# A fused linear-attention and SwiGLU kernel: the opening batch taken whole, and the hand-overs between batches rearranged

## The chip, the cores and the metric

The kernel runs on one core of a Trainium2 chip. A core has a matrix engine (PE, with its weight loads, PEld), a vector engine (DVE), an activation engine (ACT), a general engine (POOL) and a queue engine (SP); transfers between memory and the on-chip memory (SBUF) are issued from the queues of SP, ACT and POOL and moved by 16 DMA engines. Products land in PSUM, of which this program uses eight banks of 2 KB per partition. The metric is device microseconds of one execution; lower is better. Each engine works through its own instructions in the order in which the program gives them and waits on semaphores for the others.

## What is computed

Eight batches of 576 rows, eight heads of 64. For each batch and head the 64 x 64 matrix of k and v is summed over the rows, each row of q is multiplied by it, and the result is scaled to unit mean square and by g_norm. The heads side by side make 512 columns per row (4608 rows in all), and a gated feed-forward layer with its own norm follows.

```python
kv = np.einsum('bhsd,bhse->bhde', k, v)
out = np.einsum('bhsd,bhde->bhse', q, kv)
rms = np.sqrt(np.mean(out * out, axis=-1, keepdims=True) + 1e-06)
attn = out / rms * g_norm
x = attn.transpose(0, 2, 1, 3).reshape(B * S, H * D)
xn = x / np.sqrt(np.mean(x * x, axis=-1, keepdims=True) + 1e-06) * rms_g
g = xn @ w_gate
result = (g * sigmoid(g) * (xn @ w_val)) @ w_out
```

## The kernel before

Rows go through the layer in nine blocks of 512: block n below 8 is the first 512 rows of batch n ("batch n" from here on), block 8 is the eight tails of 64 rows. All products are in bf16. For a batch, `kv_products` makes the four 128 x 128 head-pair products on PE (20 matmuls, five row chunks each), `kv_copy` keeps their diagonal blocks in `kv_all`, `o` gives 128 rows of attention output (four matmuls), and from their squares `sums` forms the sum and the weighted sum for each row and head. `chain` turns both norms into one factor per row and head: twelve small DVE operations, with two steps of a root iteration. `scale` multiplies the rows by it (tile `xna`), and they are transposed into `xnt`, by four DMA transposes on SP (`x_rows`) or on PE (`x_turn`, with a copy out of PSUM).

The layer itself (`Ffn`) is 12 up units and 4 down products. `up(j)` is four matmuls into `g_ps` and four into `v_ps` (two banks each), a silu on ACT and a product on DVE into `h_sb`; `down(c)` is 12 matmuls into `o_ps`, a copy on ACT into `o_sb`, and every second time an output transfer on SP. The weights come as fp32 into staging slots (`st`, seven of 8 KB per partition, used in turn) and are rounded to bf16 by `round_w`, with the norm gain in it, and `round_wo`. q, k and v come the same way and are rounded by `cast_piece` and `cast_tail`.

The order is written out by hand: the program text is the order on every engine. Three stretches differ.

- **Opening.** Batch 0 is done in two halves of 256 rows (`Open`, q loaded in two halves). For each head pair come a cast of k on DVE, one of v on ACT, the products, two copies into `kv_all`, a product that gives the output with heads on the partitions (`outT`), and its square on ACT; sums are then tiny matmuls with the matrix `sel`. The rows are copied to SBUF (`outa`) and scaled from there. The first four up units run on the first half, then on the second, and weights are rounded between units.
- **Batch 0's down, batch 1's attention.** `wo` rounding, casts of q, the turning of q on PE, `o` and `sums` of batch 1 (squares on ACT, a product and two reductions on DVE for each tile) lie between parts of the down products. SP's queue then holds the output transfer of batch 0's first half, the loads of batch 2 (k, v, q), the second output transfer and the loads of batch 3.
- **Batches 1 to 7.** `steps` hangs work for the next batch behind each of the 16 units (0 to 11 up, 12 to 15 down): in batch 1 the chain behind unit 12, with two tiles of `x_rows` there and two behind unit 13; from batch 2 on the chain behind unit 10, and the tiles behind units 11 and 12.

On DVE the chain stands in the same queue as each unit's product into `h_sb`, which the down products read.

Of the kernel before, what the change touches and what calls it, by code (L numbers as in the profile page):

```python
# [17 lines left out]
def kernel(  # L18
# [19 lines left out]
    T = 4  # L38
# [38 lines left out]
    gnorm_bc = consts.tile([128, D], FP32, name="gnorm_bc")  # L77
# [63 lines left out]
    def load_w(blk):  # L141
        j0, j1 = W_BLOCKS[blk]
        for name, view in (("g", wg_view), ("v", wv_view)):
            st = stage()
            ap = st[:, 0 : NS * (j1 - j0) * 128].rearrange("p (s f) -> p s f", s=NS)
            nc.sync.dma_start(out=ap, in_=view[:, :, j0 * 128 : j1 * 128])
            w_st[name, blk] = ap
# [160 lines left out]
    class Ffn:  # L308
# [29 lines left out]
        def down_out(self, c):  # L338
# [10 lines left out]
            elif c % 2 == 1:  # L349
                if n == 0:  # L350
                    r0 = 256 * (c // 2)
                    rows = out[r0 : r0 + 256, :].rearrange("(p t) d -> p t d", t=2)
                else:
                    rows = out[n * S : n * S + MAIN, :].rearrange("(p t) d -> p t d", t=T)[:, c - 1 : c + 1, :]
                nc.sync.dma_start(out=rows, in_=self.o_sb)
# [6 lines left out]
    q0 = stage().rearrange("p (f h x) -> p f h x", f=2, h=H)  # L362
    k0, v0 = stage(), stage()
    raws[0, "k"], raws[0, "v"] = k0, v0

    def q0_view(f, hs):
        return q[0, hs, 256 * f : 256 * f + 256, :].rearrange("h (p t) d -> p h (t d)", t=2)

    nc.sync.dma_start(out=q0[:, 0, 0:4, :], in_=q0_view(0, slice(0, 4)))
    nc.scalar.dma_start(out=q0[:, 0, 4:8, :], in_=q0_view(0, slice(4, 8)))  # L370
    load_tail("k", k, 0, nc.sync)
    load_tail("v", v, 0, nc.scalar)
    for j in range(NS):
        hs = slice(2 * j, 2 * j + 2)
        for queue, st, src in ((nc.sync, k0, k), (nc.scalar, v0, v)):
            queue.dma_start(
                out=st.rearrange("p (h x) -> p h x", h=H)[:, hs, :], in_=main_view(src, 0)[:, hs, :]
            )
    nc.scalar.preload_act_table(ACT.Silu)
    nc.sync.dma_start(out=q0[:, 1], in_=q0_view(1, slice(0, 8)))  # L380
# [5 lines left out]
    nc.gpsimd.dma_start(out=gnorm_bc, in_=g_norm.partition_broadcast(128))  # L386
# [4 lines left out]
    nc.vector.memset(sel, 0.0)  # L391
    nc.vector.memset(kv_all, 0.0)
    for i in range(2):
        nc.vector.memset(sel[i * D : (i + 1) * D, 0, i : i + 1], 1.0 / D)
    warm_sb = consts.tile([128, 256], BF16, name="warm_sb")
    nc.vector.memset(warm_sb, 0.0)

# [4 lines left out]
    for blk in range(len(W_BLOCKS)):  # L402
        load_w(blk)

    gam_ps = att_pool.tile([128, 8], FP32, name="att_ps")
    nc.tensor.matmul(gam_ps[:, 0:5], lhsT=gam[0:5, :], rhs=ident32[0:5, 0:5], is_transpose=True, start=True, stop=True)
    nc.vector.tensor_copy(out=gcol, in_=gam_ps[:, NS : NS + 1])
    nc.vector.tensor_scalar(
        out=rowscale, in0=gam_ps[:, 0:NS], scalar1=gcol[:, 0:1], scalar2=None, op0=OP.mult
    )  # L410
    for i in range(2):
        ps_ = slice(i * D, (i + 1) * D)
        nc.vector.scalar_tensor_tensor(
            out=sel[ps_, 1, i : i + 1], in0=gcol[ps_, :], scalar=1.0 / d_model, in1=gcol[ps_, :],
            op0=OP.mult, op1=OP.mult,
        )

    alloc_q(0)
    qb0 = bufs[0]["q"]
    qt0 = qt_pool.tile([128, NS, MAIN], BF16, name="qt")  # L420

    def q0_cast(f, half, engine):
        hs = slice(4 * half, 4 * half + 4)
        cast(engine, qb0[:, 2 * f : 2 * f + 2, hs, :], q0[:, f, hs, :].rearrange("p h (t d) -> p t h d", t=2))

    def q0_turn(f, engines):
        ps = ops_pool.tile([128, NS, 2, 128], BF16, name="o_ps")
        for j in range(NS):
            for i in range(2):
                nc.tensor.matmul(  # L430
                    ps[:, j, i, :], lhsT=qb0[:, 2 * f + i, 2 * j : 2 * j + 2, :], rhs=identity,
                    is_transpose=True, start=(i == 0 and j == 0), stop=(i == 1 and j == NS - 1),
                )
        for half, engine in enumerate(engines):
            js = slice(2 * half, 2 * half + 2)
            cast(engine, qt0[:, js, 256 * f : 256 * f + 256], ps[:, js].rearrange("p j i t -> p j (i t)"))

    q0_cast(0, 0, nc.vector)
    q0_cast(0, 1, nc.vector)
    q0_turn(0, (nc.vector, nc.scalar))  # L440
    cast_tail(0, "k", nc.vector)
    cast_tail(0, "v", nc.scalar)

    class Open:
        def __init__(self, f):
            self.f = f
            self.sq = consts.tile([128, NS, 256], BF16, name=f"sqT{f}")
            self.banks = {}

        def outT(self, j):  # L450
            pool_, nm = ((gps_pool, "g_ps"), (vps_pool, "v_ps"))[j // 2]
            self.banks[j] = pool_.tile([128, MAIN], FP32, name=nm)
            nc.tensor.matmul(
                self.banks[j][:, 0:256], lhsT=kv_all[:, 0, j, :], rhs=qt0[:, j, 256 * self.f : 256 * self.f + 256],
                start=True, stop=True,
            )

        def square(self, j):
            nc.scalar.activation(out=self.sq[:, j, :], in_=self.banks[j][:, 0:256], func=ACT.Square)
# [286 lines left out]
```

## Time and profile before

| | us |
|---|---|
| three runs: median (lowest to highest) | 369.72 (366.54 to 371.88) |
| the profiled execution | 372.12 |
| its span, first to last instruction | 370.3 |
| PE busy in the span | 325.9 (88%) |
| DVE, ACT busy | 192.3, 189.3 |
| POOL busy | 8.7 |
| mean granted clock of PE | 0.97 |

The page's forty slices show where PE is not busy and where the clock falls; each digit is a tenth, a slice is 9.3 us.

```profile
PE   0567997586989799999999999999999999999995
PEld 0345643342444344445445444544454444444442
DVE  3367565256439426825781684278157716752320
ACT  1354665450656935395648556653955444513321
POOL 5000000000000000000000003000000000000000
PEclk9999998887899989999999999999999999999999
DMA  7999680029960469057715922790570153022013
```

The gaps of PE and the eights and sevens of the clock all lie in the first 14 slices, that is in the first 130 us; DMA is nearly full in the first five and again in slices 10 and 11. Rows of other views stand where the prediction uses them. In them a line gives start, duration, engine, line of the program, operation, output and inputs with their shapes, a count, and in brackets the idle time ahead and what ended it.

### The profile page before, as it was taken

The numbers are of one execution on the slowest core, as the hardware profiler recorded it, in microseconds if no ns is written. First come the engines' busy times: TensorE is split into PE (matmuls) and PEld (weight loads), VectorE is DVE, ScalarE is ACT, GpSimd is POOL, SyncE is SP. The second block draws the span as 40 slices with busy tenths as digits, with TensorE's granted clock in tenths as the row PEclk, the third lists the DMA queues.
The fourth block names the chain that finished last, engine by engine and source line by source line (L and its number), as shares of the span: only waits on it lengthen the run. The fifth ranks groups of instructions, "written<-read, shape, count | busy, mean of one in ns | idle before, by whom it ended". The sixth has DMA issues, their size and how long they took to land.

```text
span 370.3 us, 4813 instructions
## 1 busy us (share of the span) xinstructions
PE 325.9 (88%) x1717; PEld 161.6 (44%) x1749; DVE 192.3 (52%) x439; ACT 189.3 (51%) x349; POOL 8.7 (2%) x18
## 2 busy tenths in 40 slices
PE   0567997586989799999999999999999999999995
PEld 0345643342444344445445444544454444444442
DVE  3367565256439426825781684278157716752320
ACT  1354665450656935395648556653955444513321
POOL 5000000000000000000000003000000000000000
PEclk9999998887899989999999999999999999999999
DMA  7999680029960469057715922790570153022013
GB/s 180 366 339 343 207 313 17 0 73 370 379 86 3 113 170 311 4 135 210 251 25 148 337 89 58 176 354 10 139 186 19 28 153 104 1 57 115 0 25 89
DMA packets 80327, 55.39 MB, mean 150 GB/s; under 512 B 46492, under 2 KB 74144, under 8 KB 80304
## 3 DMA queue, kind: packets, MB, share of 16 engines
q1 hardware_dynamic: 78032, 53.62, 48.4%
q10 hardware_dynamic: 2144, 1.44, 1.3%
q0 software_dynamic: 128, 0.04, 0.4%
q8 instruction: 13, 0.21, 0.2%
q14 instruction: 10, 0.08, 0.1%
HBM read 37.78 MB, written 9.44 MB: 128 GB/s over the span
## 4 chain that ended last, share of the span: by engine, by line
PE 58%; DVE 11%; ACT 3%; issue 2%; SPq 2%; DMA 1%; DVEq 0%
PE v_ps L321 19%; PE g_ps L321 19%; PE o_ps L333 16%; DVE h_sb L327 3%; PE att_ps L258 2%; PE att_ps L219 2%; SPq L651 1%; DVE ssq L273 1%; ACT o_sb L341 1%; DVE sa L190 1%; DVE sc L192 1%; ACT vb L95 1%; DVE wsq L272 1%; ACT kb L95 1%; DVE sr L174 1%
## 5 line engine op out<-in xcount | busy, mean ns | idle before, releaser
L327 DVE TENSOR_TENSOR h_sb<-silu,v_ps 128x512 bf16<-128x512 bf16 (+1 forms) x112 | 74.6, 666 | 129.7 <-PE v_ps L321 79.2
L321 PE MATMUL g_ps<-xnt,wg_sb 128*128 128x512 bf16 (+1 forms) x428 | 113.7, 385 | 4.3 <-DMA xnt<-xna 2.9
L321 PE MATMUL v_ps<-xnt,wv_sb 128*128 128x512 bf16 (+1 forms) x446 | 114.9, 381 | 0.5
L333 PE MATMUL o_ps<-wo_sb,h_sb 128*128 128x512 bf16 x422 | 99.8, 390 | 10.3 <-ACT wo_sb L95 5.5
L326 ACT ACTIVATE silu<-g_ps 128x512 bf16<-128x512 f32 (+1 forms) x112 | 65.6, 586 | 76.9 <-PE g_ps L321 71.6
L333 PEld LDWEIGHTS <-h_sb 128*128 128x128 bf16 x432 | 42.5, 100 | 63.9 <-issue 11.6
L321 PEld LDWEIGHTS <-wv_sb 128*128 128x128 bf16 x448 | 45.3, 101 | 51.9 <-issue 2.8
L321 PEld LDWEIGHTS <-wg_sb 128*128 128x128 bf16 x448 | 43.5, 101 | 46.1 <-DMA xnt<-xna 3.4
L341 ACT COPY o_sb<-o_ps 128x512 f32<-128x512 f32 x36 | 21.0, 587 | 43.0 <-PE o_ps L333 42.8
L263 ACT ACTIVATE sq<-att_ps 128x512 bf16<-128x512 f32 x32 | 19.1, 598 | 23.9 <-PE att_ps L258 23.1
L273 DVE TENSOR_REDUCE ssq<-sq 128x8 f32<-128x512 bf16 x32 | 21.7, 679 | 0.0
L274 DVE TENSOR_REDUCE wssq<-wsq 128x8 f32<-128x512 bf16 x32 | 21.6, 676 | 0.0
L283 DVE TENSOR_TENSOR xna<-outa,sy 128x512 bf16<-128x512 bf16 x32 | 19.9, 685 | 0.1
L265 ACT CAST outa<-att_ps 128x512 bf16<-128x512 f32 x32 | 18.6, 582 | 0.0
L95 ACT CAST vb<-st 128x512 bf16<-128x512 f32 x32 | 18.5, 615 | 0.0
L272 DVE TENSOR_TENSOR wsq<-sq,gsq 128x512 bf16<-128x512 bf16 x32 | 13.4, 419 | 4.3 <-ACT sq L263 4.3
L95 ACT CAST qb<-st 128x512 bf16<-128x512 f32 x26 | 14.3, 618 | 1.7 <-DMA st<-in_q_dram 1.7
L219 PE MATMUL att_ps<-vb,kb 128*128 128x128 bf16 x140 | 10.3, 219 | 2.2 <-DVE kb L97 1.3
L258 PEld LDWEIGHTS <-qt 128*128 128x128 bf16 x112 | 9.0, 102 | 6.5 <-issue 0.6
L219 PEld LDWEIGHTS <-kb 128*128 128x128 bf16 x140 | 9.0, 98 | 5.7 <-DVE kb L97 1.5
L258 PE MATMUL att_ps<-kv_all,qt 128*128 128x128 bf16 x112 | 11.2, 226 | 0.0
L95 ACT CAST kb<-st 128x512 bf16<-128x512 f32 x20 | 10.9, 619 | 0.0
(94 smaller groups left out, 137.2 us busy)
## 6 DMA issues: line engine op xcount, KB each, us to landing
out_dram<-o_sb SPq DMA_DIRECT2D x16, 512.0 KB, 3.1
st<-in_k_dram SPq DMA_DIRECT2D x7, 1024.0 KB, 8.5
st<-in_v_dram SPq DMA_DIRECT2D x7, 1024.0 KB, 8.8
st<-in_q_dram SPq DMA_DIRECT2D x7, 1024.0 KB, 6.6
st<-in_moe_w_out_dram SPq DMA_DIRECT2D x3, 1024.0 KB, 6.1
st<-in_moe_w_gate_dram SPq DMA_DIRECT2D x2, 1024.0 KB, 6.4
st<-in_moe_w_val_dram SPq DMA_DIRECT2D x2, 1024.0 KB, 6.2
rawt<-in_k_dram SPq DMA_DIRECT2D x8, 128.0 KB, 8.2
```

Of the source, the lines that this page charges most:

```text
L95: engine.copy(out=dst, in_=src)
L219: nc.tensor.matmul(self.kv_ps[:, j, :], lhsT=bufs[n]["k"][:, c, hs, :], rhs=bufs[n]["v"][:, c, hs, :], start=(j == 0 and c == 0), stop=(j ...
L258: nc.tensor.matmul(ps[:, 2 * j : 2 * j + 2, :], lhsT=a, rhs=b, start=(j == 0 and i == 0), stop=(j == NS - 1 and i == len(terms) - 1),)
L263: nc.scalar.activation(out=self.sq, in_=ps, func=ACT.Square)
L273: nc.vector.reduce_sum(out=self.ssq[:, c, :], in_=self.sq, axis=AX.X)
L274: nc.vector.reduce_sum(out=self.wssq[:, c, :], in_=wsq, axis=AX.X)
L283: nc.vector.tensor_tensor(out=self.xna[c], in0=self.outa[c], in1=self.alpha[:, c, :].to_broadcast([128, H, D]), op=OP.mult)
L321: nc.tensor.matmul(ps[:, 0:w], lhsT=wt[:, s, j * 128 : (j + 1) * 128], rhs=x[:, s, lo:hi], start=(s == 0), stop=(s == NS - 1),)
L326: nc.scalar.activation(out=silu[:, 0:w], in_=g_ps[:, 0:w], func=ACT.Silu)
L327: nc.vector.tensor_tensor(out=self.h[:, j, lo:hi], in0=silu[:, 0:w], in1=v_ps[:, 0:w], op=OP.mult)
L333: nc.tensor.matmul(self.o_ps[c], lhsT=self.h[:, j, c * 128 : (c + 1) * 128], rhs=wo_sb[:, j, :], start=(j == 0), stop=(j == NF - 1),)
L341: nc.scalar.copy(out=self.o_sb[:, c % 2, :], in_=self.o_ps[c])
```

## The change

It touches seven places.

1. **Loads.** q, k and v of batch 0 come in the layout of all other batches, by pieces of four and two heads instead of two (q's pieces were 512 bytes wide, now 1024); the two smallest weight blocks share one staging slot each for gate and value, so that two slots are freed; batch 1's q is asked for before `wo`.
2. **Opening whole.** `Early` replaces `Open`: all 512 rows of q are turned at once, products over 512 columns for squares, one set of sums, one chain of 32 columns. A mask and one multiplication replace two copies into `kv_all`. `scale` reads the rows from PSUM; `outa` is gone here.
3. **Casts issued ahead.** ACT casts the next v ahead of a square. Sixteen idle matmuls (`warm`) follow the last `o`. Up units 0 and 1 run on 128, 128 and 256 rows; the rest on 512.
4. **Roundings.** Value block 0 and block 1 go to POOL; block 2 is rounded in one run ahead of unit 2, block 3 in units 4 to 6; k and v of batch 1 are cast in units 7 to 10, q on POOL.
5. **Second batch by products.** Batch 1 takes its sums as batch 0 does (`out_turned`, `square`, `sums`) and scales from PSUM, its `o` in the `g_ps` and `v_ps` banks; `wo` is rounded by ACT and DVE (block 0), POOL and DVE (1), POOL and ACT (2).
6. **Batch 1's steps.** Casts for batch 2 by a table (q and k in the first two units, v after), `o` and `sums` one unit earlier.
7. **The chain.** In every batch from 1 on, chain, the four scales and the four DMA transposes stand behind up unit 11.

```diff
     def load_w(blk):
         j0, j1 = W_BLOCKS[blk]
+        size = NS * (j1 - j0) * 128
+        shared = stage() if size <= 1024 else None
...
+        def out_turned(self, j, pool_, name):
+            ps = pool_.tile([128, MAIN], FP32, name=name)
+            nc.tensor.matmul(ps, lhsT=kv_all[:, self.n, j, :], rhs=self.qt[:, j, :], start=True, stop=True)
+            return ps
...
+        def scale(self, c):
+            self.xs[c] = xna_pool.tile([128, H, D], BF16, name="xna")
+            nc.vector.tensor_tensor(
+                out=self.xs[c], in0=self.o_ps[c], in1=self.alpha[:, c, :].to_broadcast([128, H, D]), op=OP.mult
+            )
...
+    for s in range(NS):
+        round_w(0, "v", s, nc.gpsimd)
+    for name in "gv":
+        for s in range(NS):
+            round_w(1, name, s, nc.gpsimd)
+    warm(vps_pool.tile([128, MAIN], FP32, name="v_ps"), 16)
...
+    ffn = Ffn(0)
+    load_batch(1, "kvq")
+    for c in range(3):
+        first.scale(c)
+        if c < 2:
+            first.turn((c,), ops_pool, "o_ps", nc.scalar)
+        if c == 0:
+            p = Up(ffn, 0, 0, 128)
+            p.products()
+            p.silu()
...
+    att.kv_products((0, 1))
+    att.kv_products((2, 3))
+    att.kv_copy()
+    round_wo(0, 0, nc.scalar)
+    round_wo(0, 1, nc.vector)
+    att.q_turn(0, nc.scalar)
+    att.q_turn(1, nc.vector)
+    second.qt = att.qt
+    for c in range(2):
+        ffn.down_products(c, 0, 4)
+    round_wo(1, 0, nc.gpsimd)
+    round_wo(1, 1, nc.vector)
+    for j in range(NS):
+        second.square(j, second.out_turned(j, att_pool, "att_ps"))
+    for c in range(2):
+        ffn.down_products(c, 4, 8)
+    round_wo(2, 0, nc.gpsimd)
+    round_wo(2, 1, nc.scalar)
+    for j in range(NS):
+        second.sums(j, att_pool, "att_ps")
+    second.chain()
+    for c in range(T):
+        second.o(c, *(((gps_pool, "g_ps"), (vps_pool, "v_ps"))[c // 2]))
+    for c in range(2):
+        ffn.down_products(c, 8, NF)
+    for c in range(2):
+        ffn.down_out(c)
+    ffn.down_products(2, 0, NF)
...
+            plan = {
+                0: ("q0", "q1", "k0", "k1"),
+                1: ("q2", "q3", "k2", "k3"),
+                2: ("v0", "v1", "k4"),
...
-            steps[10] += [nxt.chain]
-            for c in range(2):
+            steps[11].append(nxt.chain)
+            for c in range(T):
                 steps[11] += [lambda c=c: nxt.scale(c), lambda c=c: nxt.x_rows(c)]
-                steps[12] += [lambda c=c: nxt.scale(2 + c), lambda c=c: nxt.x_rows(2 + c)]
```

What this does to the order is shown at three places; a row is line, operation, output and inputs with the tile names used above. First ACT in the opening, from its first cast on. Before:

```order
L95 COPY qt<-o_ps 128x2x256
L95 CAST vb_119<-rawt 64x512
L95 CAST vb_119<-st 128x4x128
L459 ACTIVATE sqT_205<-g_ps 128x256
L95 CAST vb_119<-st 128x4x128
L459 ACTIVATE sqT_205<-g_ps 128x256
L95 CAST vb_119<-st 128x4x128
L459 ACTIVATE sqT_205<-v_ps 128x256
L95 CAST vb_119<-st 128x4x128
L459 ACTIVATE sqT_205<-v_ps 128x256
L481 CAST outa<-o_ps 128x512 x2
```

And now:

```order
L99 CAST qb<-st 128x4x256
L99 CAST vb_123<-rawt 64x512
L99 CAST vb_123<-st 128x4x128
L99 COPY qt<-o_ps 128x1024
L99 CAST vb_123<-st 128x4x128
L425 ACTIVATE sqT<-g_ps 128x512
L99 CAST vb_123<-st 128x4x128
L425 ACTIVATE sqT<-g_ps 128x512
L99 CAST vb_123<-st 128x4x128
L425 ACTIVATE sqT<-v_ps 128x512 x2
L160 ACTIVATE wg_sb<-st,rowscale 128x256 x4
```

The cast of the second piece of v has moved ahead of the first square, and each later cast likewise; half of q's cast and of its copy has come to ACT, and the copies of the rows are gone.

Second, POOL from its last fill of the opening (`vb`) to the fill of the staging slots for the tails of q. Before:

```order
L390 MEMSET kb_117 64x512
L390 MEMSET kb_118 64x512
L390 MEMSET vb_119 64x512
L390 MEMSET vb_120 64x512
L644 MEMSET st 64x2048 x2
```

And now:

```order
L392 MEMSET vb_124 64x512
L162 TENSOR_SCALAR wv_sb<-st,rowscale 128x256 x4
L162 TENSOR_SCALAR wg_sb<-st,rowscale 128x256 x4
L162 TENSOR_SCALAR wv_sb<-st,rowscale 128x256 x4
L101 CAST qb<-st 128x4x128 x4
L101 CAST wo_sb<-st 128x1024 x2
L715 MEMSET st 64x2048 x2
```

POOL, which had no arithmetic, has twelve roundings, four casts of q and two of `wo`.

Third, DVE at the end of a batch's up units, batch 2 as an example: the end of the chain and what follows it, before,

```order
L190 TENSOR_TENSOR sa_1555<-sy_1553 128x32
L192 SCALAR_TENSOR_TENSOR sc_1557<-sa_1555,sz 128x32
L194 SCALAR_TENSOR_TENSOR sy_1559<-sc_1557,sy_1553 128x32
L327 TENSOR_TENSOR h_sb<-silu,v_ps 128x512
L283 TENSOR_TENSOR xna<-outa,sy_1559 128x512 x4
```

and now the last two products into `h_sb` and the start of the chain:

```order
L333 TENSOR_TENSOR h_sb<-silu,v_ps 128x512 x2
L284 TENSOR_SCALAR u<-ssq 128x32
L180 RECIPROCAL sr<-u 128x32
L182 TENSOR_TENSOR st<-sr,wssq 128x32
L184 TENSOR_REDUCE sm<-st 128x4
```

The product of the last up unit has moved from behind the chain to ahead of it.

On SP the output transfer of batch 0's first half still stands ahead of the loads of batch 2, in the same order as before; in batch 1 the four DMA transposes of `xnt` now stand together, where an output transfer parted them.

More of the change, by code (lines that the diff above doesn't have):

```diff
@@ L418 @@
[L418 to L436, printed above, removed]
@@ L518 @@
             )
[L519 to L529 removed]
+        nc.vector.tensor_tensor(out=kv_all[:, 0, j, :], in0=ps, in1=mask, op=OP.mult)
+    cast_piece(0, "v", 1, nc.scalar)
@@ L530 @@
+    first.sums(0, gps_pool, "g_ps")
+    first.sums(1)
+    first.sums(2)
+    first.o(0, ops_pool, "o_ps")
+    first.o(1, ops_pool, "o_ps")
+    first.sums(3)
+    first.chain()
+    first.o(2, att_pool, "att_ps")
+    first.o(3, att_pool, "att_ps")
     for s in range(NS):
         round_w(0, "g", s, nc.scalar)
-    for j in range(NS):
-        Bh.outT(j)
-    A.rows((nc.vector, nc.vector))
     for s in range(NS):
-        round_w(0, "v", s, nc.vector)
-    for j in range(NS):
-        Bh.square(j)
@@ L580 @@
+    for i in range(4):
+        cast_piece(1, "q", i, nc.gpsimd)
     att.kv_products((0, 1))
```

385 lines of the change are left out of this document (203 added, 182 removed).

## Prediction

> **What bounds the kernel now.** I read first the busy time by stage, with cuts where batch 0's first up unit starts, where its last one ends, and where batches 1, 2 and 8 start.
>
> ```profile
> core 0: us, PE busy (x) PEld busy (x) DVE busy (x) ACT busy (x) POOL busy (x), PEclk, DMA share, GB/s
> 0.00:29.40 29.40, 12.50 (x97) 9.19 (x98) 14.17 (x50) 11.01 (x24) 5.07 (x16) 1.00 0.94 299
> 29.40:57.70 28.30, 25.91 (x137) 15.03 (x138) 17.30 (x47) 16.94 (x35) 0.00 (x0) 1.00 0.79 267
> 57.70:90.30 32.60, 20.82 (x116) 10.50 (x116) 17.53 (x40) 12.64 (x22) 0.00 (x0) 0.82 0.31 99
> 90.30:130.00 39.70, 35.69 (x176) 16.64 (x179) 21.03 (x47) 25.36 (x48) 0.00 (x0) 0.93 0.56 158
> 130.00:334.50 204.50, 199.74 (x1055) 96.22 (x1077) 114.00 (x245) 113.21 (x206) 3.60 (x2) 0.99 0.48 136
> ```
>
> From 130 us on PE is the bound: 199.74 of 204.50 us for six batches, 34.1 each. The 130 us ahead hold only two batches, and PE's busy time in them is swollen by a slow clock. So I read PE's timeline next.
>
> ```profile
> 31.17 1.06 PE L321 MATMUL g_ps<-xnt,wg_sb 128*128 128x256 bf16 x4
> 42.04 0.60 PE L321 MATMUL g_ps<-xnt,wg_sb 128*128 128x256 bf16 x4
> 42.48 0.60 PE L321 MATMUL v_ps<-xnt,wv_sb 128*128 128x256 bf16 x4
> 59.47 1.07 PE L219 MATMUL att_ps<-vb,kb 128*128 128x128 bf16 x16 [1.29 <-DVE kb L97]
> 61.94 3.25 PE L333 MATMUL o_ps<-wo_sb,h_sb 128*128 128x512 bf16 x8 [1.40 <-ACT wo_sb L95]
> 67.67 3.15 PE L333 MATMUL o_ps<-wo_sb,h_sb 128*128 128x512 bf16 x7 [2.04 <-ACT wo_sb L95]
> ```
>
> At 42 us groups of four 256-column products start 0.44 us apart, so a whole up unit (eight products of 512) costs 1.73. The same group at 31.17 takes 1.06: half speed, although the first stages' granted clock of 1.00 does not show it. At 61.94 eight down products need 3.25 us instead of 1.73: behind the waits of 1.29 and 1.40 the clock has fallen (0.82 in the third stage). A wait here costs twice.
>
> Third, what ends those waits, and what holds batches 1 and 2:
>
> ```profile
> 14.38 0.61 ACT L95 CAST vb<-st 128x512 bf16<-128x512 f32 x1
> 15.04 0.69 PE L516 MATMUL att_ps<-vb,kb 128*128 128x128 bf16 x5 [0.66 <-ACT vb L95]
> 17.66 0.69 PE L516 MATMUL att_ps<-vb,kb 128*128 128x128 bf16 x5 [0.66 <-ACT vb L95]
> 35.35 1.21 PE L500 MATMUL att_ps<-identity,xna 128*128 128x128 bf16 x8 [2.27 <-DVE xna L493]
> 80.01 0.36 SPq L355 DMA_DIRECT2D out_dram<-o_sb  x1
> 90.36 1.86 PE L321 MATMUL g_ps<-xnt,wg_sb 128*128 128x512 bf16 x4 [0.78 <-DVE xnt L97]
> 94.54 1.66 ACT L95 CAST qb<-st 128x512 bf16<-128x512 f32 x3 [1.68 <-DMA st<-in_q_dram]
> 130.10 1.89 PE L321 MATMUL g_ps<-xnt,wg_sb 128*128 128x512 bf16 x4 [2.90 <-DMA xnt<-xna]
> ```
>
> The opening is a ring of 2.6 us per head pair (15.04 to 17.66): ACT casts the next v only after the last square. At 35.35 PE stands 2.27 us for the second half's rows. Batch 2's loads stand on SP behind the first output transfer (80.01), and their last, q, is cast from 94.54, 14.5 us later, ending a wait of ACT.
>
> **The change, part by part.** Durations and transfers for it:
>
> ```profile
> 0.00:9.00 9.00, 0.23 (x1) 0.18 (x1) 3.03 (x11) 1.28 (x1) 5.07 (x16) 1.00 0.81 181
> 9.00:42.00 33.00, 22.59 (x152) 16.32 (x153) 18.30 (x67) 15.41 (x36) 0.00 (x0) 1.00 1.01 345
> L154 ACT ACTIVATE wg_sb<-st,rowscale 128x512 bf16<-128x512 f32 x8 | 5.7, 715 | 0.0
> L95 ACT CAST wo_sb<-st 128x1024 bf16<-128x1024 f32 x3 | 3.1, 1049 | 0.0
> L95 ACT COPY qt<-att_ps 128x1024 bf16<-128x1024 bf16 x1 | 1.0, 1012 | 2.7 <-PE att_ps L243 2.7
> L493 DVE TENSOR_TENSOR xna<-outa,oy 128x512 bf16<-128x512 bf16 x4 | 2.6, 686 | 0.1
> masks.py:199 POOL TENSOR_SCALAR_AFFINE_SELECT identity<-identity 128x128 bf16<-128x128 bf16 x1 | 0.3, 287 | 0.1
> masks.py:199 POOL TENSOR_SCALAR_AFFINE_SELECT ident<-ident 8x8 f32<-8x8 f32 x1 | 0.2, 182 | 0.1
> ```
>
> *The loads.* 181 GB/s to 9 us are 1.6 MB, then 345 GB/s. q, the tails and the first halves of k and v (2.3 MB) are there at 10.9 us, all three (3.4 MB) at 14, the first weights (4.4 MB) at 17.0, the second (5.5) at 20.2, all weights at 33, batch 1 at 43, wo at 46, 49 and 52. I give the wider pieces no better rate: the bound below is none, above it the 345 from the start, 4 us earlier. Batch 1's q now stands ahead of wo on SP; wo is wanted from 52 us on, so that costs nothing.
>
> *Opening to the last up unit.* ACT now does v0, qt's second half, v1, square 0, v2, square 1, v3, squares 2 and 3. From 10.8: 0.61, 1.01, 0.61 bring v1 to 13.0; kv 1 ends at 13.8, the first product over 512 columns at 14.4, and squares (0.60) and casts alternate to 16.8. kv 3 waits for kv 2's copy and k3 on DVE, runs 17.4 to 18.1, then copy, product, square: 19.7. Twelve sums and two o tiles on the slow clock (0.69 for five, above) end at 21.5, the last sums at 21.9. The chain takes 2.72 us (187.52 to 190.24 below): 24.9. The 16 `warm` products (3.4 us at half speed) fill PE meanwhile. I add 1.5 for POOL beside the chain (rival b): 26.4. Then a tile of rows takes scale 0.69, turn 0.4 and copy 0.6, and narrow up units lie between: the first 256-wide unit starts 5.5 later, at 31.9. Two of those (0.87 each, if the clock is up) and units 2 and 3 end at 37.1; ACT rounds four pieces (2.9 us) ahead of two silus, so unit 4 waits 0.2; eight units end at 51.1, where the old kernel had 57.7. At nothing, since DVE and ACT wait there: the gammas behind kv 0, the mask product for two copies, outa's copies dropped, g_norm squared by a product.
>
> *POOL* takes 12 roundings of 256 columns, 4 casts of 512, 2 of 1024: 28 times one rounding. No row shows one. From 8 to 128 elements an operation grows by 105 ns, so 256 make 0.40; if two multiplies cost two passes and nothing is fixed, 1.15. It is one instruction on one input as the row is: I take 0.45. The eight of block 1 then end at 23.8 and are wanted at 33.6.
>
> *From there to batch 1.* k and v are cast in units 7 to 10, so the 20 products run at once. Behind the last unit ACT does silu, kv copy and half of wo (0.6, 0.36, 1.05, with hops 2.9): down starts at 54.0, and two turns lie before it. Then eight products 1.73; four out products and squares, where two att banks make PE wait (1.8 in all); 1.73; 16 sums 1.0; o 0.9; 1.73; the first output copy. With hops the first transfer leaves 12.7 after the last unit, at 63.8 instead of 80.01. Dropped are wsq, two reductions and outa for each tile; two wo halves go to POOL, which waits for nothing. Down 2 (2.6) covers chain and scale; turns 0.9, down 3 2.6: batch 1's unit 0 starts at 69.2, not 90.36.
>
> *Batch 1 then waits.* q of batch 2 still comes 14.5 after the output transfer, 78.3. ACT stands before its cast in unit 0; behind it silu 1 ends at 78.3 + 1.2 + 0.6 = 80.1. PE has done units 0 to 2 by 74.4, idles 5.7, and its clock falls: 2.0 (at 130.10 four products take 1.89, not 0.87). With 9 units 15.6, kv and o 2.0, v's tail 0.5 and down 10.4 it ends at 110.6; 1.5 more for one spell of half clock between 27 and 64: 112.1. Before it was 130.10 less 2.90, 127.2. Gain 15.1.
>
> *The later transitions.*
>
> ```profile
> 117.46 0.68 DVE L327 TENSOR_TENSOR h_sb<-silu,v_ps 128x512 bf16<-128x512 bf16 x1
> 119.58 0.18 DVE L278 TENSOR_SCALAR u<-ssq 128x32 f32<-128x32 f32 x1
> 126.40 2.54 SPq L290 DMA_TRANSPOSE xnt<-xna  x2
> 187.52 0.17 DVE L278 TENSOR_SCALAR u<-ssq 128x32 f32<-128x32 f32 x1
> 190.24 0.68 DVE L327 TENSOR_TENSOR h_sb<-silu,v_ps 128x512 bf16<-128x512 bf16 x1
> 190.98 8.16 PE L333 MATMUL o_ps<-wo_sb,h_sb 128*128 128x512 bf16 x36 [0.47 <-DVE h_sb L327]
> 191.59 5.15 SPq L290 DMA_TRANSPOSE xnt<-xna  x4
> 198.98 1.03 PE L321 MATMUL g_ps<-xnt,wg_sb 128*128 128x512 bf16 x4
> ```
>
> Into batch 2 the chain starts behind h (117.46 + 0.6), not at 119.58: 1.5 earlier; and no output transfer parts the four transposing transfers: 0.6. The wait of 2.90 falls to 0.8, too short for the clock to fall (1.6): 3.7 in all. In the six later ones h ahead of the chain takes away PE's 0.47, but xna comes 0.73 later: the last transfer starts at 191.59 + 3.9 + 0.7 and lands 2.4 after (half-way through the pair at 126.40, 127.7, to PE's start at 130.10), 198.6, where PE is ready at 198.5. It gives 0.2 back: 0.27 a time, 1.6.
>
> *The sum:* 372.1 (span 370.3 and what lies around it) less 15.1, 3.7 and 1.6 is 351.7. The median, 369.72, stands 2.4 lower: **349.3**.
>
> **The rivals.** (a) *q of batch 2 does not hold PE.* For it: DMA is idle before it; against: the same bytes took 14.5. Without the 5.7 and its 2: 341.6. (b) *POOL and DVE hold each other up.* Eight operations of the chain read one or two tiles in SBUF alone while POOL rounds; if each waits for one rounding (0.40 to 0.9), the chain grows by 3.2 to 7.2 rather than 1.5: 351 to 355. No row has both reading. The Trainium skill, SBUF — State Buffer, section Who interferes with whom, says this: a VectorE operation with two SBUF inputs and a reading GpSimd one lock each other out for a whole instruction. (c) *The clock stays low from 51 to 67,* as from 62 to 79. 13 us of products would double, less 4 behind the chain and the 1.5 counted: 357. For it: short products; against: gaps of 1 us and less, where 1.3 to 2 threw it. The Trainium skill, TensorE: Matmul & The Clock Gate, section What's actually happening, wants one busy window of about 3.4 us for the full clock; the trace agrees: the products from 29.4 to the gap (35.35 less 2.27), 3.7 us, kept half speed. (d) *POOL becomes the bound:* the slower side. wo's last half is wanted at 58; from 18 us 28 pieces fit up to 1.4 us each, and every 0.1 beyond costs 2.8 us. At 2.13 all 20.4 are eaten; at 2.5 it is 380. Against: 287 ns for half a piece. (e) *The moved chain gives all back* in later batches: 351.
>
> **How the numbers follow.** The forecast with (e) 0.60, (a) 0.12, (b) 0.13, (c) 0.11, (d) 0.04. The range goes from (a) less 2.6 for an earlier opening to (c) plus 3 for hops I have missed, 339 to 360, and leaves out (d) and about 0.1 of times gone astray. 2% is 7.4 us, about what a measurement here can tell, and 362.3 the border: faster 0.91, same 0.05, slower 0.04.
>
> **What would show it.** Right: first output transfer near 64; after batch 1's third unit a PE gap of about 5 us, ended by a silu behind the q casts; under 1 us of wait into batch 2; no 0.47 in later downs. Wrong: POOL pieces above 1.1 us, gaps in the first chain, batch 0's down products 0.43 us apart.

## The result, and the profile after

The changed kernel takes 356.17 us (median of three runs, 355.00 to 356.37) against 369.72; the ratio is 0.963 with a 95% interval of 0.952 to 0.975. Five more rounds of it beside the kernel before gave 355.69 against 371.08, a ratio of 0.959 (0.955 to 0.963). The gain is 13.6 us by the first medians and 15.4 by the second. The ratios leave out a kernel's runs that lie over 1.5% above its fastest one, the medians leave out none. The forecast was 349.3, so the time lies inside the range and about 7 us above the number.

The first view is the time by stage of the profiled execution after (355.0 us, span 353.2). The cuts are the first up unit on 256 rows, the end of batch 0's up units, and the starts of batches 1, 2 and 8; the last batch's stage is left out. The columns are those of the same view in the prediction.

```profile
0.00:28.46 28.46, 16.99 (x150) 12.55 (x151) 13.42 (x43) 12.82 (x24) 11.04 (x28) 1.00 1.00 324
28.46:48.75 20.29, 19.31 (x98) 9.41 (x97) 13.97 (x30) 13.67 (x26) 3.51 (x5) 1.00 1.07 346
48.75:66.00 17.25, 16.10 (x138) 9.35 (x137) 9.17 (x22) 8.00 (x13) 1.24 (x2) 1.00 0.21 71
66.00:110.93 44.93, 35.25 (x182) 16.33 (x181) 21.00 (x46) 25.51 (x49) 0.00 (x0) 0.92 0.70 176
110.93:317.26 206.33, 200.89 (x1076) 96.48 (x1077) 115.04 (x245) 114.09 (x208) 3.60 (x2) 0.99 0.53 135
```

Batch 0's down and batch 1's attention (the third row) took 32.60 us at a granted clock of 0.82 before and take 17.25 at 1.00 now; PE is idle in it for 1.2 us instead of 11.8, and its busy time is 4.7 shorter. The fourth row is the weak one: PE works 35.25 of 44.93 us. The fifth holds six batches in 206.33 us, where the same six took 204.51 before (130.10 to 334.61): they became *longer*. PE's timeline shows the places.

```profile
34.79 0.20 PE L621 MATMUL att_ps<-gsq,ones 1*128 1x64 bf16 x1 [0.98 <-DVE gsq L618]
55.18 1.89 PE L339 MATMUL o_ps<-wo_sb,h_sb 128*128 128x512 bf16 x8
79.32 1.86 PE L327 MATMUL g_ps<-xnt,wg_sb 128*128 128x512 bf16 x4 [7.98 <-ACT silu L332]
110.93 1.02 PE L327 MATMUL g_ps<-xnt,wg_sb 128*128 128x512 bf16 x4 [1.33 <-DMA xnt<-xna]
144.97 1.02 PE L327 MATMUL g_ps<-xnt,wg_sb 128*128 128x512 bf16 x4 [0.79 <-DMA xnt<-xna]
279.61 1.02 PE L327 MATMUL g_ps<-xnt,wg_sb 128*128 128x512 bf16 x4 [0.43 <-DMA xnt<-xna]
287.66 0.93 PE L264 MATMUL att_ps<-kv_all,st 128*128 128x128 bf16 x7 [2.65 <-DMA st<-st]
```

At 55.18 eight down products take 1.89 us, where they took 3.25 before. Four waits stand here. The product that spreads g_norm squared makes PE wait 0.98. In batch 1 PE stands 7.98 us for a silu that ACT issues behind q's casts, and then runs at half speed (the unit from 79.32 to 82.55 takes 3.23 us instead of 1.73). Into batch 3 PE waits 0.79 us for the transposed rows, and into each later batch some 0.4, as at 279.61, where it used to wait 0.47 in the down products. And in batch 7 it waits 2.65 us for the turned q tails (tile `st`), again with half speed behind it. Starts of unit 0, read from the two traces:

| batch | 1 | 2 | 3 | 7 | 8 | end |
|---|---|---|---|---|---|---|
| before | 90.36 | 130.10 | 165.24 | 300.16 | 334.61 | 370.3 |
| after | 66.00 | 110.93 | 144.97 | 279.61 | 317.26 | 353.2 |
| ahead | 24.36 | 19.17 | 20.27 | 20.55 | 17.35 | 17.1 |

24.4 us were won before batch 1, 5.2 given back in it, and 3.2 in batch 7. By the stage rows, 0.9 of the 24.4 lie before the first unit on 256 rows, 8.0 in batch 0's up units and 15.4 in its down. Two parts of the change that act there were taken out again in the runs below (the idle products, POOL's share); the others ahead of batch 1 were not taken out one by one, so what each is worth there is read from traces and not shown by a run. In SP's queue and on PE, batch 7's hand-over was this in the kernel before:

```profile
292.77 5.14 SPq L290 DMA_TRANSPOSE xnt<-xna  x4
298.64 10.41 SPq L651 DMA_TRANSPOSE st<-st  x8
306.33 0.56 PE L258 MATMUL att_ps<-kv_all,st 128*128 128x128 bf16 x7 [0.77 <-DMA st<-st]
```

and in the kernel after:

```profile
273.12 5.14 SPq L296 DMA_TRANSPOSE xnt<-xna  x4
278.98 11.49 SPq L722 DMA_TRANSPOSE st<-st  x8
```

Counted from unit 0 of batch 7, the rows' four transfers start 7.39 us ahead before (292.77 to 300.16) and 6.49 ahead after, and the eight that turn the tails stand behind them: they start 1.52 and 0.63 ahead.

### The profile page after: what moved, and what is told of

Same layout as the page of the kernel before. It is cut to its first block, busy times and chain, and to the rows that moved or that the text cites. A ratio compares the mean times of both kernels' runs of the same rounds, so it can differ in the third digit from the quotient of the medians.

```text
span 353.2 us, 4868 instructions
## 1 busy us (share of the span) xinstructions
PE 319.8 (91%) x1782; PEld 158.1 (45%) x1782; DVE 180.9 (51%) x398; ACT 183.9 (52%) x333; POOL 19.4 (5%) x36
## 4 chain that ended last, share of the span: by engine, by line
PE 65%; DVE 13%; DMA 11%; SPq 6%; ACT 2%; issue 2%; DVEq 0%; ACTq 0%
PE g_ps L327 24%; PE v_ps L327 23%; PE o_ps L339 9%; DVE xna L289 4%; SPq L296 4%; DMA xnt<-xna 3%; DMA st<-in_k_dram 3%; DMA st<-in_q_dram 3%; DVE h_sb L333 2%; PE att_ps L264 2%; PE att_ps L225 2%; DMA qt<-qb 2%; SPq L722 1%; PE v_ps L406 1%; DMA st<-st 1%
## 5 line engine op out<-in xcount | busy, mean ns | idle before, releaser
L333 DVE TENSOR_TENSOR h_sb<-silu,v_ps 128x512 bf16<-128x512 bf16 (+2 forms) x109 | 73.6, 676 | 131.6 <-PE v_ps L327 120.9
L327 PE MATMUL g_ps<-xnt,wg_sb 128*128 128x512 bf16 (+2 forms) x436 | 112.1, 380 | 12.3 <-ACT silu L332 8.0
L327 PE MATMUL v_ps<-xnt,wv_sb 128*128 128x512 bf16 (+2 forms) x436 | 111.4, 378 | 0.0
L332 ACT ACTIVATE silu<-g_ps 128x512 bf16<-128x512 f32 (+2 forms) x109 | 64.7, 594 | 70.2 <-PE g_ps L327 70.2
L339 PE MATMUL o_ps<-wo_sb,h_sb 128*128 128x512 bf16 x432 | 95.4, 379 | 0.1
L327 PEld LDWEIGHTS <-wg_sb 128*128 128x128 bf16 x436 | 40.6, 99 | 55.4 <-issue 15.7
L99 ACT CAST qb<-st 128x512 bf16<-128x512 f32 (+1 forms) x25 | 14.2, 636 | 11.7 <-DMA st<-in_q_dram 11.7
L279 DVE TENSOR_REDUCE ssq<-sq 128x8 f32<-128x512 bf16 x28 | 19.0, 678 | 0.0
L280 DVE TENSOR_REDUCE wssq<-wsq 128x8 f32<-128x512 bf16 x28 | 18.9, 675 | 0.0
L715 POOL MEMSET st<- 64x2048 bf16 x2 | 3.6, 1800 | 156.2 <-ACT qb L99 155.4
```

What stands on the lines that cost most here:

```text
L99: engine.copy(out=dst, in_=src)
L279: nc.vector.reduce_sum(out=self.ssq[:, c, :], in_=self.sq, axis=AX.X)
L280: nc.vector.reduce_sum(out=self.wssq[:, c, :], in_=wsq, axis=AX.X)
L327: nc.tensor.matmul(ps[:, 0:w], lhsT=wt[:, s, j * 128 : (j + 1) * 128], rhs=x[:, s, lo:hi], start=(s == 0), stop=(s == NS - 1),)
L332: nc.scalar.activation(out=silu[:, 0:w], in_=g_ps[:, 0:w], func=ACT.Silu)
L333: nc.vector.tensor_tensor(out=self.h[:, j, lo:hi], in0=silu[:, 0:w], in1=v_ps[:, 0:w], op=OP.mult)
```

## The experiments

All were timed in five rounds beside the kernel before. Where a run is set against "the changed kernel", that is 355.69 us. Not all runs stood in the same set of rounds; the kernel before had 371.33, 371.08 and 371.48 us in the three sets.

**The chain put back in the later batches (e1).**

```diff
-            steps[11].append(nxt.chain)
-            for c in range(T):
+            steps[10].append(nxt.chain)
+            for c in range(2):
                 steps[11] += [lambda c=c: nxt.scale(c), lambda c=c: nxt.x_rows(c)]
+                steps[12] += [lambda c=c: nxt.scale(2 + c), lambda c=c: nxt.x_rows(2 + c)]
```

> The changed kernel, with the root chain of batches 3 to 8 and of the tails back behind up unit 10 (two rows' transfers behind unit 11, two behind the first down unit, as before). Theory A (the moved chain gives time back): the transposing transfers of rows leave SP 0.9 us later there, and in the second-to-last block the eight transfers that turn the q tails stand behind them, so the wait of 2.65 us for the turned tails falls back to about 0.8 and the half-speed clock behind it (about 1 us) goes; at the five other transitions a wait of 0.35 to 0.44 for a transfer is exchanged for the old one of 0.47 for h_sb. Sum: about 3 us less, 353 against 356.2. Theory B (the tails' transfers themselves are slower, 1.44 us each against 1.30, for another reason): the wait stays above 1.7 and the time within 1.5 us of the changed kernel's.

352.43 us (351.55 to 352.72), 3.3 less. PE's waits in this run:

```profile
272.11 8.16 PE L339 MATMUL o_ps<-wo_sb,h_sb 128*128 128x512 bf16 x37 [0.47 <-DVE h_sb L333]
286.40 0.56 PE L264 MATMUL att_ps<-kv_all,st 128*128 128x128 bf16 x7 [0.89 <-DMA st<-st]
```

The 0.47 is back at each transition, the wait for the tails is 0.89, and the products behind it run at full speed (seven in 0.56, not 0.93). Theory A holds: this part of the change costs about 3 us. Its eight transfers of tails took 11.45 us together, as slow as after, so theory B's slower transfers alone do not make the loss.

**The chain moved in the kernel before, and nothing else (e2).**

```diff
-            steps[10] += [nxt.chain]
-            for c in range(2):
+            steps[11] += [nxt.chain]
+            for c in range(T):
                 steps[11] += [lambda c=c: nxt.scale(c), lambda c=c: nxt.x_rows(c)]
-                steps[12] += [lambda c=c: nxt.scale(2 + c), lambda c=c: nxt.x_rows(2 + c)]
```

> The kernel before, with only this part of the change: the root chain of batches 3 to 8 and of the tails behind up unit 11 and all four rows with it. Theory A: the 0.47 us waits for h_sb go, waits of about 0.4 us for the transposing transfers come, and the wait for the turned q tails grows from 0.77 to about 2.6 with 1 us of half-speed clock behind it: about 2.5 us slower than the kernel before, 372. The prediction's own step: 0.27 us gained at each of six transitions, 1.6 us faster, 368.

372.05 us against 371.33, a ratio of 1.0057 (1.0014 to 1.0099). The medians differ by 0.7 us, the interval of the ratio is 0.5 to 3.7 us slower: theory A's 2.5 lies in it, and the 1.6 us of gain that the prediction took do not. In the two traces the stretch from batch 2's first unit to the end is 0.7 longer (240.9 against 240.2).

```profile
305.25 0.56 PE L258 MATMUL att_ps<-kv_all,st 128*128 128x128 bf16 x7 [1.78 <-DMA st<-st]
```

The transitions trade 0.47 for 0.33 to 0.36 in five cases (0.64 in the sixth). The wait for the tails grows by 1.0, as the later start says, and in this execution the clock stays up behind it. The other 0.9 us of the changed kernel's wait do not follow from the start of these transfers (in e8 below, with the same start of 0.62 us ahead of unit 0, PE waits 1.79). They belong to the fifth transfer, for which PE waits. It leaves SP here, and in the kernel after, at

```profile
302.86 1.20 SPq L651 DMA_TRANSPOSE st<-st  x1
284.33 1.20 SPq L722 DMA_TRANSPOSE st<-st  x1
```

and PE's product starts 2.4 us later here (305.25) and 3.3 later in the kernel after (287.66). In e1, e7 and e8 this time is 2.5 us, in e4, e5 and e6 it is 3.3 to 3.5; what makes the difference is not shown.

**The tails turned in the order in which they are read (e3).** PE's first tail product reads row tile 0 of both halves; the program issues all four tiles of one half first.

```diff
-                for c in range(T):
+            for c in range(T):
+                for u in range(2):
                     steps[NF + 2].append(lambda u=u, c=c: turn_q_tails(u, c))
```

> The changed kernel, with the eight transfers that turn the q tails issued in the order in which they are read (both halves of row tile 0 first, not all four of one half and then the other). Theory A: PE waited for the fifth of eight in a row of 1.44 us each; now it needs the second, there about 283 us where the product stands at 284.8, so the wait of 2.65 goes and the clock stays up: about 3.7 us less, 352.5. Rival: PE waits for all eight, or for the transfers ahead of them: no change.

351.88 us (350.59 to 352.63), 3.8 less. The eight products of row tile 0 run without a wait:

```profile
286.00 0.61 PE L264 MATMUL att_ps<-kv_all,st 128*128 128x128 bf16 x8
```

The wait was that of the fifth transfer in the queue, not of the eight together; the rival falls.

**Batch 2's loads ahead of the first output transfer (e4).** The line `load_batch(2)` goes from ahead of batch 0's last down product to behind the four casts of batch 1's q.

```diff
         cast_piece(1, "q", i, nc.gpsimd)
+    load_batch(2)
     att.kv_products((0, 1))
...
-    load_batch(2)
     ffn.down_products(3, 0, NF)
```

> The changed kernel, with the loads of batch 2 issued on SP behind the loads of wo (batch 0's last up units), not behind the first output transfer. Theory A (the 8.0 us gap in batch 1 is made by where these loads stand on SP; the DMA engines are idle from 52 to 60 us): q is there by 63, no wait for silu in batch 1, no half-speed clock behind it: 8.0 and about 1.8 less, 346.5. Rival B (the loads take the bandwidth from wo's loads or the buffers come free too late): down of batch 0 waits for wo instead, 351 or more. Rival C: the gap goes, but the shorter batch 1 waits at batch 2's first unit for its rows: 348 to 350.

349.07 us (346.93 to 349.98), 6.6 less, not 9.2. SP's queue and PE in this run:

```profile
52.68 1.14 SPq L116 DMA_DIRECT2D st<-in_q_dram  x1
72.46 3.48 SPq L108 DMA_DIRECT2D rawt<-in_v_dram  x1
76.05 6.64 SPq L238 DMA_TRANSPOSE qt<-qb  x4
82.50 0.40 PE L264 MATMUL att_ps<-kv_all,qt 128*128 128x128 bf16 x4 [2.69 <-DMA qt<-qb]
```

q of batch 2 now leaves SP at 52.68 instead of 68.72, the wait of 7.98 is gone, and batch 2 starts 7.0 us earlier (103.89). That DMA time was free: from 52 to 60 us the DMA share is 0.00 in the kernel after and 1.08 here, and batch 1 still starts at 66.19 (66.00 after), so wo's loads lost nothing and rival B falls. The place in SP's queue made the gap. But a new wait of 2.69 appears, at another place than rival C named: the four transfers that turn q stand behind batch 3's loads, which hold SP from 67.41 to 75.94. So theory A is right in its cause and short by a wait that lay behind the first.

**Without the idle products (e6).** The line `warm(..., 16)` behind the opening's last `o` is left out; those products feed nothing.

> The changed kernel without the 16 products of 256 columns that fill TensorE during the first root chain (they feed nothing). Theory A (they bring the clock up): the narrow units and part of the wide ones run at half speed, as before (1.06 for four products of 256 columns, not 0.60): some 8 groups more at half speed, of which the narrow ones hide beside the scales; 1.5 to 3 us longer. Rival B: scales, turns and copies set that stretch and the clock is up by then anyway: no difference, within 0.5.

357.71 us (356.65 to 359.94), 2.0 more. In the kernel after the rows' first turn and the first unit run at full speed, 0.39 and 0.38 for four products of 128; without the idle products:

```profile
24.74 0.61 PE L459 MATMUL o_ps<-identity,xna 128*128 128x128 bf16 x4 [3.19 <-DVE xna L451]
26.02 0.59 PE L566 MATMUL g_ps<-xnt,wg_sb 128*128 128x128 bf16 x4 [0.67 <-ACT xnt L99]
28.53 0.39 PE L566 MATMUL g_ps<-xnt,wg_sb 128*128 128x128 bf16 x4
```

Full speed comes at 28.5, where the kernel after has it from 24.4. Theory A holds in direction and size. In the traces the first unit on 256 rows starts at 30.04, against 29.06 in e5 (and 28.46 in the first profiled execution), so about 1 of the 2.0 us is seen at this place; the rest was not found.

**GpSimd's work on VectorE (e8).** Five arguments `nc.gpsimd` (block 0's values, block 1, batch 1's q, two halves of `wo`) become `nc.vector`.

> The changed kernel, with what GpSimd rounds and casts (12 pieces of weights, batch 1's q, two halves of wo) on VectorE at the same places. Theory A (GpSimd's share is worth its while): 12 pieces of about 0.28 stand between the first chain and the first scale, four q casts of 0.42 before the copy of kv, two halves of wo before the second batch's chain: 3.3 - 0.5 (the chain is no longer held up, 2.72 instead of 3.28) + 1.7 + 1 = 4 to 6 us longer, 361. Theory B (VectorE loses beside a working GpSimd what that one takes over: its casts took 0.75 instead of 0.42 there): within 1.5 us of the changed kernel.

358.22 us (356.65 to 359.26), 2.5 more, between the two theories. The chain in the kernel after starts at 20.35 (its first row, `u`) and ends where the scales start; the fifth of its operations to the seventh, and the first scales:

```profile
21.41 0.19 DVE L186 SCALAR_TENSOR_TENSOR sz<-sm,u 128x32 f32<-128x32 f32 x1
21.63 0.37 DVE L190 TENSOR_SCALAR syi<-sz 128x32 int32<-128x32 int32 x1
22.04 0.42 DVE L196 TENSOR_TENSOR sa<-syi 128x32 f32<-128x32 f32 x1
23.63 1.29 DVE L451 TENSOR_TENSOR xna<-o_ps,sy 128x512 bf16<-128x512 f32 x2
```

and with POOL idle:

```profile
22.20 0.18 DVE L190 TENSOR_SCALAR syi<-sz 128x32 int32<-128x32 int32 x1
22.42 0.19 DVE L196 TENSOR_TENSOR sa<-syi 128x32 f32<-128x32 f32 x1
23.66 1.13 DVE L162 TENSOR_SCALAR wv_sb<-st,rowscale 128x256 bf16<-128x256 f32 x4
26.81 1.28 DVE L451 TENSOR_TENSOR xna<-o_ps,sy 128x512 bf16<-128x512 f32 x2
```

The chain took 3.28 us beside POOL's roundings (20.35 to 23.63) and takes 2.73 without (20.93 to 23.66): POOL's work costs it 0.55. The twelve pieces cost VectorE 3.15 (23.66 to 26.81), and batch 2 starts 3.6 us later than in the profiled execution of e5 (116.16 against 112.60). The end is only 1.0 us later in the same two executions, since the wait for the tails happened to be 1.79 instead of 2.71 and full speed followed it.

**The chain cut in two (e7).** `chain` is split behind `yi`: its first six operations behind unit 10, the two root steps behind unit 11. This holds from batch 3 on; into batch 2 both parts stay behind unit 11. The line of the edit that does it:

```diff
-            steps[11].append(nxt.chain)
+            steps[10].append(nxt.chain)
+            steps[11].append(nxt.chain_rest)
```

> The changed kernel, with the root chain of batches 3 to 8 and of the tails cut in two: its first six operations (1.4 us) behind up unit 10, the six of the two Newton steps behind unit 11. Theory A: rows leave 1.3 us earlier and h_sb of unit 11 is not delayed past its use, so both waits (0.35 to 0.44 for the rows here, 0.47 for h_sb before) vanish at six transitions, 2.3 us, and the wait for the turned q tails falls from 2.65 to about 1.3 with less half-speed clock: 3.5 to 5 us less in all, about 352. Rival: the first half delays h_sb of unit 11 and the 0.47 comes back: 353 or 354.

349.81 us (348.07 to 350.83), 5.9 less, more than theory A's 3.5 to 5. Against the trace of e5, batches 2 to 6 are 0.5 to 0.6 us shorter each, more than the waits of 0.35 to 0.47 that theory A counted, and batch 7 is 3.8 shorter (38.44 to 34.61). In the list of PE's waits neither the 0.47 for `h_sb` nor the 0.4 for rows is left at the later transitions (one of 0.22 is), and the tails:

```profile
284.36 0.56 PE L272 MATMUL att_ps<-kv_all,st 128*128 128x128 bf16 x7 [1.56 <-DMA st<-st]
```

wait 1.56, with full speed behind it. So moving the chain was the wrong half of a good idea: behind unit 11 it spares `h_sb`, behind unit 10 it spares the rows, and half and half spares both.

**The corrections together (e9).** Loads, tails and split chain as above, batch 3's loads behind the four transfers of batch 2's q, and the product for g_norm squared one unit behind its VectorE operation.

> The changed kernel with four corrections: batch 2's loads behind wo's (and batch 3's behind the four transfers that turn batch 2's q, so that these do not stand behind them on SP), the q tails turned in the order in which they are read, the chain of later batches cut in two, and the product that spreads g_norm squared issued one up unit after the VectorE operation that it waits for. Theory A (each removes a wait of its own on PE and the sum adds up): 355.7 less 3.8 (tails), 2.2 (six transitions), 9.3 (6.6 as measured alone, 2.7 for the wait for the turned q that was left) and 1.0 is 339.4. Rival B: a wait that is removed comes back later (batch 2's first unit waits longer for its rows, batch 3's loads come late): 343 or more.

336.42 us (335.50 to 337.53), a ratio to the kernel before of 0.913 (0.907 to 0.918): 19.3 less than the changed kernel. Each correction keeps its gain beside the others, so theory A holds; it is even 3 us more than the sum of the parts. By the starts of unit 0 in the profiled pair (355.0 and 336.4 us), 1.0 is won ahead of batch 1, 10.0 in it (the sum had 9.3) and 7.5 in batches 2 to 7 (the sum had 2.2 and 3.8); the rest is the distance of the changed kernel's profiled execution from its median (355.0 against 355.7).

**And batch 2's work one unit sooner (e10).** The edit is against e9; the cast of v's tail, which goes from ACT in unit 4 to VectorE in unit 3, is left out here.

```diff
-            steps[4] += [lambda: nxt.kv_products((0, 1))]
-            steps[5] += [lambda: nxt.kv_products((2, 3)), nxt.kv_copy]
+            steps[4] += [lambda: nxt.kv_products((0, 1)), lambda: nxt.kv_products((2, 3)), nxt.kv_copy]
             for c in range(T):
-                steps[6 + c].append(lambda c=c: nxt.o(c))
-                steps[7 + c].append(lambda c=c: nxt.sums(c))
-            steps[11] += [nxt.chain, nxt.chain_rest]
+                steps[5 + c].append(lambda c=c: nxt.o(c))
+                steps[6 + c].append(lambda c=c: nxt.sums(c))
+            steps[10].append(nxt.chain)
+            steps[11].append(nxt.chain_rest)
```

> The kernel of e9, with batch 2's kv products in one unit behind up unit 4 of batch 1 (v's tail cast on VectorE), its out and sums one unit earlier each, and its chain cut in two behind units 10 and 11, as in later batches. Theory A: the last wait for rows, 1.3 us at batch 2's first unit, shrinks to 0.2: 1 us less than e9. Rival: PE waits for v's casts behind unit 4 instead (ACT has two casts of 0.6 and a silu of 0.6 in units of 1.73): no difference.

335.11 us (335.03 to 335.58), a ratio of 0.909 (0.904 to 0.914), 1.3 less than e9: the fastest kernel of the study. Batch 2's first unit no longer waits for its rows, as theory A says, and batch 1 is 1.5 us shorter (33.35 against 34.89); but a wait that e9 does not have comes at batch 3's first unit, and batch 2 is 0.75 longer.

```profile
132.53 1.02 PE L338 MATMUL g_ps<-xnt,wg_sb 128*128 128x512 bf16 x4 [0.89 <-DMA xnt<-xna]
```

Its time by stage from the narrow units on, cut near the starts of batches 1, 2 and 8, shows PE at work in nearly all of it and the clock at 1.00 throughout:

```profile
25.00:65.50 40.50, 38.34 (x279) 21.50 (x280) 24.86 (x58) 24.95 (x46) 5.15 (x6) 1.00 0.98 307
65.50:99.50 34.00, 33.68 (x181) 16.30 (x184) 21.06 (x47) 24.80 (x48) 0.00 (x0) 1.00 0.57 162
99.50:298.00 198.50, 196.52 (x1052) 95.71 (x1072) 113.93 (x245) 113.69 (x208) 3.60 (x2) 1.00 0.56 139
```

**The changed kernel once more (e5).**

> The changed kernel itself once more, beside the others. Theory A: its median is 355 to 357, and what lies between the forecast's difference and the measured one is in the traces. Theory B: the kernel before scatters by several us from run to run, so part of it is scatter; then this median differs from 356.2 by more than 1 us, or the median of before does from 369.7.

355.69 us, within 0.5 of the first measurement; the kernel before had 371.08 in the same rounds and scatters more (366.27 to 374.23 over all rounds). So the changed kernel's time stands, and 1.4 of the 2.4 us by which the prediction moved its sum down to a median were scatter of three runs.

## Why the prediction was right and where it failed

The direction and the range held. Step by step, in the profiled pair (372.1 and 355.0):

| step of the prediction | forecast | measured |
|---|---|---|
| first unit on 256 rows | 31.9 | 28.46 |
| batch 0's up units end | 51.1 | 48.75 |
| first output transfer | 63.8 | 60.73 |
| batch 1's first unit | 69.2 | 66.00 |
| gain to the end of PE's work in batch 1 | 15.1 | 17.6 |
| gain at batch 2's first unit and from the slow clock behind it | 3.7 | 3.0 |
| gain at the six later transitions, with all that follows | 1.6 | -3.5 |
| sum | 20.4 | 17.1 |

Errors of both signs stand in this sum: up to batch 3 the gain is 1.8 us above the forecast, behind that 5.1 below it. That they cancel in part is luck.

*The opening, the up units and batch 0's down* ran in the order worked out, and 3.2 us early. The last kv products of the opening start at 17.32 (forecast 17.4); the chain starts at 20.35, 1.85 before the forecast's 22.2 (24.9 less 2.72), so the products, squares and sums between took 3.0 and not 4.8. Rival (b), for which I had added 1.5, cost 0.55. From the first 256-wide unit to the end of the up units I had 19.2; it took 20.29, and the wait of 0.98 for the g_norm product, which I had put at nothing, is nearly all of the difference: in e9, with that product moved, the stretch takes 19.25 (28.74 to 47.99). The 128x256 piece on POOL took 0.46 (four in 1.85 us) against my 0.45, so rival (d) never came near. Rival (c) did not happen: in the third stage eight down products take 1.89 us and not 3.25. Nor did the one spell of half clock for which the sum had 1.5.

*Batch 1's wait* was the right mechanism and somewhat too small. I carried over 14.5 us from output transfer to q's cast, and it took 16.9; PE stood 7.98, not 5.7, so rival (a) falls. In the rows after:

```profile
60.73 0.36 SPq L357 DMA_DIRECT2D out_dram<-o_sb  x1
64.19 4.43 SPq L108 DMA_DIRECT2D rawt<-in_v_dram  x1
68.72 1.01 SPq L116 DMA_DIRECT2D st<-in_q_dram  x1
77.63 1.14 ACT L99 CAST qb<-st 128x512 bf16<-128x512 f32 x2 [9.98 <-DMA st<-in_q_dram]
```

From q's issue to its cast it is 8.9 us, as before (85.40 to 94.54, 9.1). What is more lies ahead of it: SP needed 8.0 us to issue what stands before q, 4.43 of them for v's tail, where it had needed 5.4 before (80.01 to 85.40). e4 shows that the gap was made by the place in the queue. The slow clock behind it cost 1.5 us (3.23 instead of 1.73 for a unit), where I had 2.0. That the gain to the end of batch 1 is 2.5 above the forecast, although the gap was 2.3 longer, comes from the 3.2 of the early start and the 1.5 that were not needed.

*The step that failed* is "In the six later ones h ahead of the chain takes away PE's 0.47, but xna comes 0.73 later ... It gives 0.2 back: 0.27 a time, 1.6." The 0.47 went, as said. But the rows' transfers give back 0.79 into batch 3 and 0.35 to 0.44 later, where I had 0.2: the first transition lost 0.3, and the next four gained 0.28 together. And I followed the moved step only to PE's next unit. On SP the eight transfers of the q tails stand behind the rows. In the kernel before PE already waited 0.77 us for them, so there was no slack, and a later start counts in full: in e2 they start 1.0 us later and PE waits 1.0 longer. In the kernel after the wait grows by 1.88 (0.77 to 2.65), half of it by the later start and half by the longer fifth transfer, and the products behind it at half speed cost another 1.4: 3.2 us in batch 7, with 0.1 the other way. e1, e2 and e3 show from three sides that the moved chain and the order of these transfers make the loss. Rival (e) had the place and the direction but too small a price: it took away the 1.6, and the runs took away 5.1. The last 0.25 us of this, in the last batch, were not placed.

*Into batch 2* the wait fell from 2.90 to 1.33, where I had 0.8, so this sign of being right, under 1 us, failed. The spell of slow clock behind it was worth 1.4, not 1.6 (the unit at 130.10 took 3.14 us before instead of 1.73). This spell is the 8 in the fifteenth of the clock's slices at the start: not all low digits lie in the first 14.

The rest of the distance to the medians is scatter: the profiled execution of before stood 2.4 above its median of three, that of the changed kernel 1.2 below its own.

## What to carry to other kernels

When a step is moved later, list everything behind it on each queue it issues to, for every iteration with an extra load on that queue, and look for a consumer that already waits: there the delay is paid in full. Where one order makes a product late and the other a transfer, see whether the step can be cut in two. A gap that a load's place in a queue makes can be removed by asking for the load earlier, as here where the DMA engines stood idle ahead of it; but look at what comes behind the moved load on the same queue, which may have to be moved too.

## What the runs showed of the hardware that was not expected

*The same gap does and does not lower the clock.* In the changed kernel, PE's wait for the tails of 2.65 us left the next seven 128-column products at 0.93, half speed; in e5 one of 2.71 did the same. In e6 a longer wait at the same place, 2.79, left full speed behind it: these products take 0.56, and the units after them 1.73 each. The 2.69 in batch 1 of e4, quoted above, also left full speed. A third case lies between: behind e4's wait for the tails of 2.67 the seven products run at full speed, and half speed comes 1.3 us after PE has resumed, at 282.07. The rows of e6, then of e4:

```profile
289.51 0.56 PE L264 MATMUL att_ps<-kv_all,st 128*128 128x128 bf16 x7 [2.79 <-DMA st<-st]
280.77 0.56 PE L264 MATMUL att_ps<-kv_all,st 128*128 128x128 bf16 x7 [2.67 <-DMA st<-st]
282.07 1.91 PE L327 MATMUL v_ps<-xnt,wv_sb 128*128 128x512 bf16 x4
```

The length of a gap alone does not decide, and the products just behind it do not tell whether the clock will fall. The Trainium skill, TensorE: Matmul & The Clock Gate, section What's actually happening, says that the clock follows PE's activity in windows of about 3.4 us that run freely, so that the moment of the change depends on where in a window the work lands; these cases agree with that. It gives one idle window as what it takes to fall back; here 2.65 us were enough. The 3.7 us of products at half speed that the prediction counts as agreeing decide nothing: with windows that run freely, such a stretch need not hold a whole one. Gaps like these were paid for in some runs and not in others.

*VectorE beside GpSimd.* While POOL casts q, VectorE casts k of batch 1. The rows of POOL and VectorE in the kernel after:

```profile
42.57 2.67 POOL L101 CAST qb<-st 128x512 bf16<-128x512 f32 x4 [20.14 <-DMA st<-in_q_dram]
42.72 1.50 DVE L101 CAST kb<-st 128x512 bf16<-128x512 f32 x2
```

and VectorE's row with POOL idle, in e8:

```profile
46.94 0.75 DVE L101 CAST kb<-st 128x512 bf16<-128x512 f32 x2
```

Two casts took twice as long beside POOL. In the chain it was different: its first five operations ran beside POOL's roundings (which lasted until 22.43) at the durations they have elsewhere, and only the next two were held up. The Trainium skill, SBUF — State Buffer, section Who interferes with whom, names casts and `tensor_scalar` in their two-port modes, and operations with two SBUF inputs, as those of VectorE that contend with a reading GpSimd. The casts agree, and so do the two that were held up, `syi` (a `tensor_scalar`, 0.37 instead of 0.18) and `sa` (two inputs, 0.42 instead of 0.19). `sz`, with two inputs in SBUF, took its usual 0.19 here, so not every such operation was held up.
